# The last token group's products with w_out, taken with tokens on partitions and stored by two queues

## The chip, the cores and the metric

The kernel runs on 1 core of one Trainium2 chip. The metric is device time in microseconds (us) of one execution, lower is better. Before the change the median of 4 runs is 301.98 us (301.85 to 302.33). The profile belongs to one of these runs: it took 302.33 us, of which the profiled span, from the first to the last instruction, is 300.1 us.

## The reference

Two blocks follow each other. The first is a kernelised attention with batch 4, 4 heads, 1088 positions and head size 32: q and k are mapped to 64 features each by an outer product of two small projections, and keys, values and queries are combined through a 64 x 32 matrix per head. Its output, laid out as 4352 tokens of 128 features, is the input x of the second block, a feed-forward layer with 2048 hidden units:

```python
def phi(x):
    a = np.einsum('rd,bhsd->bhsr', S1, x)
    b = np.einsum('rd,bhsd->bhsr', S2, x)
    return np.einsum('bhsi,bhsj->bhsij', a, b).reshape(*x.shape[:-1], r * r)
q_p, k_p = (phi(q), phi(k))
...
h = x @ w_in                                   # 4352 x 128 times 128 x 2048
g = np.where(h > 0.0, h, np.exp(np.minimum(h, 0.0)) - 1.0)
return (g @ w_out).astype(np.float32)          # 2048 x 128
```

## The kernel before

**Tokens and groups.** A sequence of 1088 positions is read as 64 rows y of 17 neighbours t, so position = 17 y + t. A "half tile" is one (batch b, t) with its 64 rows y; there are 4 x 17 = 68 of them. They are taken in 9 groups: groups 0 to 7 have 8 half tiles (512 tokens, as 4 tiles of 128), the last group, g = 8, has 4 half tiles, that is 256 tokens in 2 tiles of 128 (`qn[8] = 2`). In each 128-token tile the upper 64 partitions (u = 0) hold one half tile and the lower 64 (u = 1) another.

**The feed-forward stage.** It takes nearly the whole span. The 2048 hidden units are 16 chunks of 128, worked in 8 pairs (`cp`, `NP = 8`). For each group and pair there is a step:

- `mm1` (L492): two products with w_in give h, hidden units on partitions and tokens on columns, in two PSUM tiles (tag `h`, 4 buffers, line 496). The 128 x 128 piece of w_in is the stationary operand (the one loaded into the array), the group's x (`xg`) the moving one (streamed through).
- `elu` (L514): per chunk, ScalarE makes relu(-h) and exp(-that) (L504, L505), and VectorE combines it with h to `gg` (L511), in SBUF, hidden units on partitions.
- `mm2` (L519): two products with w_out (L525) add into one PSUM tile `o` of the group (tag `o`, one buffer), output features on partitions and tokens on columns. Here too the 128 x 128 piece of `W` is stationary and `gg` (512 columns, 256 in the last group) is moving.

Every float32 product is carried out in two passes, each a weight load and a matmul in the trace; so one `mm2` call has 4 passes.

**The order of the work** is written out by hand: the schedule is manual, and each engine executes its instructions in the order of the emission. The loop over `n` at the end emits `mm1` of step n, then small work of other stages (`extra`), then `elu` of step n, then `mm2` of step n - 2. After the last `mm1` three calls of `mm2` therefore follow each other. Waits between engines go by semaphores that the framework places from the tiles that are read and written, and on TensorE the wait stands ahead of the weight load.

**The end of a group.** `fin1` (L530) takes `o` when its 8 pairs are summed. For groups 0 to 7 VectorE transposes `o` in blocks of 32 x 32 into `ob` (L545) and SyncE's queue stores it in 16 or more small transfers (L551). The last group goes another way: VectorE copies `o` to SBUF as `oT` (L541), and two rounds of the loop later `fin2` (L553) has TensorE transpose its two 128 x 128 tiles (L557) into a PSUM tile of tag `aux`, ScalarE copies that to `osb` (L559), and SyncE's queue issues two transfers, one per half u, of 64 rows of 1 KB (L563): for each y, the 2 neighbouring tokens t, t+1 with 128 features each are contiguous in the output.

Of the kernel before, what the change touches and what calls it, by code (L numbers as in the profile page):

```python
# [12 lines left out]
F32 = mybir.dt.float32  # L13
# [14 lines left out]
def kernel(  # L28
# [18 lines left out]
    nc = tc.nc  # L47
    B, H, S, D = q.shape
    R = S1.shape[0]
    P = 128  # L50
# [3 lines left out]
    NP = NC // 2  # L54
# [7 lines left out]
    work = ctx.enter_context(tc.tile_pool(name="wk", bufs=2))  # L62
    psum = ctx.enter_context(tc.tile_pool(name="psum", bufs=2, space=bass.MemoryType.PSUM))
# [83 lines left out]
    W = const.tile([P, NP, 4 * P], F32, name="W")  # L147
# [49 lines left out]
    ident = const.tile([P, P], F32, name="ident")  # L197
# [138 lines left out]
    NQ = (NH + 7) // 8  # L336
    qn = [min(8, NH - 8 * g) // 2 for g in range(NQ)]
# [5 lines left out]
    def half_tile(g, i, u):  # L343
        return divmod(8 * g + u * qn[g] + i, NT)

    def runs(g, u, i0, i1, step=1):

        i = i0
        while i < i1:
            b, t = half_tile(g, i, u)  # L350
            m = 1
            while i + m * step < i1 and half_tile(g, i + m * step, u)[0] == b:
                m += 1
            yield b, t, i, m
            i += m * step
# [134 lines left out]
    hs, es, gs, ops = {}, {}, {}, {}  # L490

    def mm1(g, cp):  # L492
        n = qn[g] * P
        hs[g, cp] = [psum.tile([P, 512], F32, name="h", tag="h", bufs=4) for c in range(2)]
        for c in range(2):
            nc.tensor.matmul(hs[g, cp][c][:, :n], W[:, cp, c * P:c * P + P], xg[g][:, :n])  # L496
# [17 lines left out]
    def elu(g, cp):  # L514
        for c in range(2):
            elu_a(g, cp, c)
            elu_d(g, cp, c)

    def mm2(g, cp, first, last):  # L519
        n = qn[g] * P  # L520
        if first:
            ops[g] = psum.tile([P, 512], F32, name="o", tag="o", bufs=1)
        gg = gs.pop((g, cp))
        for c in range(2):
            nc.tensor.matmul(ops[g][:, :n], W[:, cp, (2 + c) * P:(3 + c) * P], gg[:, c, :n],  # L525
                             start=(first and c == 0), stop=(last and c == 1))

    oT = {}

    def fin1(g, last):  # L530
        n = qn[g] * P
        o = ops.pop(g)[:, :n]
        if g in oT:
            nc.vector.tensor_add(oT[g][:, :n], oT[g][:, :n], o)
            o = oT[g][:, :n]
        elif not last:
            oT[g] = work.tile([P, 512], F32, name="oT", tag="oT")
            nc.scalar.copy(oT[g][:, :n], o)  # L538
        if last and g == NQ - 1:
            oT[g] = work.tile([P, 512], F32, name="oT", tag="oT")  # L540
            nc.vector.tensor_copy(oT[g][:, :n], o)  # L541
        elif last:

            ob = work.tile([P, 4, 2, 2, D], F32, name="ob", tag="ob", bufs=2)
            nc.vector.transpose(ob[:].rearrange("p i u w d -> p (i u w) d"), o)  # L545
            rows = out.rearrange("(b w y t) (q d) -> b w q y t d", b=B, w=2, t=NT, q=4)
            for u in range(2):
                for b, t, i, m in runs(g, u, 0, qn[g]):
                    for w in range(2):
                        for q_ in range(4):  # L550
                            nc.sync.dma_start(rows[b, w, q_, :, t:t + m, :], ob[32 * q_:32 * q_ + 32, i:i + m, u, w, :])  # L551

    def fin2(g):  # L553
        n = qn[g]
        p = psum.tile([P, 512], F32, name="otp", tag="aux")
        for i in range(n):
            nc.tensor.transpose(p[:, i * P:i * P + P], oT[g][:, i * P:i * P + P], ident[:])  # L557
        o = work.tile([P, 4, P], F32, name="osb", tag="osb", bufs=1)
        nc.scalar.copy(o[:, :n].rearrange("p t f -> p (t f)"), p[:, :n * P])  # L559
        rows = out.rearrange("(b y t) f -> b y t f", b=B, t=NT)  # L560
        for u in range(2):
            for b, t, i, m in runs(g, u, 0, n):
                nc.sync.dma_start(rows[b, :, t:t + m, :], o[64 * u:64 * u + 64, i:i + m, :])  # L563


    keep_warm(2)
# [66 lines left out]
    for b in range(1, B):  # L633

        n = NP - 2 if b == 1 else NP * (b * NT // 8 - 2) + 1
# [10 lines left out]
    for g in range(2, NQ):  # L646
        n = NP * (g - 1) + (g == 2)
# [2 lines left out]
        at(n + 5, q4, g)  # L650
        at(n + 6, q5, g)

    done = {}
    N = len(steps)
    for n in range(N + 4):
        if 2 <= n < N:
            g, cp, first, last = steps[n]
            mm1(g, cp)
        for f, *a in extra.get(n, ()):
            f(*a)  # L660
        if 2 <= n < N:
            elu(g, cp)
        for f, *a in extra.get((n, 1), ()):
            f(*a)
        if 2 <= n < N + 2:
            g, cp, first, last = steps[n - 2]
            mm2(g, cp, first, last)
            if last:
                fin1(g, cp == NP - 1)
                if cp == NP - 1 and g == NQ - 1:  # L670
                    done[n + 2] = g
        if n in done:
            fin2(done[n])


# [27 lines left out]
```

## Time and profile before

| what | value |
|---|---|
| median of 4 runs | 301.98 us (301.85 to 302.33) |
| the profiled execution | 302.33 us, its span 300.1 us |
| TensorE matmul busy | 288.3 us, 96% of the span, 1454 passes |
| VectorE, ScalarE busy | 168.8 us (56%), 188.1 us (63%) |
| products with w_out, L525 | 288 passes, 130.7 us; of these 32 passes of 256 columns in the last group, 8.0 us |
| last pass of L525 ends, VectorE's copy starts | 295.24 us after the start of the span |
| the two last stores are issued | at 296.60 and 297.19 us |

The profile is one execution recorded by the hardware. Times in its views are in us from the start of the span unless they are marked ns. Engines are PE (TensorE's matmuls), PEld (TensorE's weight loads, which overlap PE), DVE (VectorE), ACT (ScalarE), POOL (GpSimd) and SP (SyncE); a q behind a name is its queue of waits and DMA issues. A duration of one matmul in the trace is its latency, from the first column in to the last result out, so neighbours overlap; the distance from start to start is the pace.

### The profile page before, as it was taken

How to read it: one execution, taken by the hardware profiler on the slowest of the kernel's cores; microseconds unless marked ns; L12 is line 12 of the kernel's file. 1: busy time of each engine (PE TensorE's matmuls, PEld its weight loads, DVE VectorE, ACT ScalarE, POOL GpSimd, SP SyncE). 2: the span in 40 equal slices, each digit the busy share in tenths (PEclk: the TensorE clock that was granted, in tenths of full speed). 3: DMA queues.
4: the chain of work that ended last, by engine and by line, in shares of the span. 5: the costliest groups of instructions: out<-in, count | busy, mean ns of one | idle time of the engine just before them, and what ended most of it. 6: DMA issues, size and time to landing. Idle time of an engine off the chain costs nothing.

```text
span 300.1 us, 4046 instructions
## 1 busy us (share of the span) xinstructions
PE 288.3 (96%) x1454; PEld 147.8 (49%) x1454; DVE 168.8 (56%) x297; ACT 188.1 (63%) x354; POOL 18.5 (6%) x45
## 2 busy tenths in 40 slices
PE   8887999999998999999998999999999999999994
PEld 5763335544444654445544654444444534444682
DVE  5788899963765384436356275436443644354441
ACT  1526797566666268746667268656774687568682
POOL 2010024440000010000000010000000000000000
PEclk9999999999999999999999999999999999999998
DMA  6932899620020100001000200001001000110020
GB/s 188 331 127 73 182 209 215 61 74 0 7 31 0 29 9 0 2 9 27 2 1 4 33 0 0 0 15 23 0 0 24 14 0 1 15 22 0 3 33 17
DMA packets 38291, 13.37 MB, mean 45 GB/s; under 512 B 32768, under 2 KB 36480, under 8 KB 38272
## 3 DMA queue, kind: packets, MB, share of 16 engines
q1 hardware_dynamic: 37984, 12.86, 19.7%
q10 hardware_dynamic: 288, 0.26, 0.3%
q8 instruction: 11, 0.18, 0.2%
q14 instruction: 8, 0.07, 0.1%
HBM read 10.88 MB, written 2.23 MB: 44 GB/s over the span
## 4 chain that ended last, share of the span: by engine, by line
PE 92%; ACT 3%; DVE 3%; issue 1%; DVEq 0%
PE o L525 39%; PE h L496 37%; PE kv L296 3%; PE xps L475 2%; PE abp L269 2%; PE idle L216 2%; PE qtp L460 2%; PE abwp L363 2%; ACT e L505 1%; ACT e L504 1%; ACT ab L273 1%; PE x0ps L427 1%; DVE qp L384 0%; PE abqp L394 0%; DVE gg L511 0%
## 5 line engine op out<-in xcount | busy, mean ns | idle before, releaser
L511 DVE SCALAR_TENSOR_TENSOR gg<-e,h 128x512 f32<-128x512 f32 (+1 forms) x144 | 93.0, 656 | 105.8 <-ACT e L505 105.6
L525 PE MATMUL o<-gg,W 128*128 128x512 f32 (+1 forms) x288 | 130.7, 577 | 1.3 <-ACT oT L538 0.7
L496 PE MATMUL h<-xg,W 128*128 128x512 f32 (+1 forms) x288 | 128.8, 569 | 1.8 <-DVE xg L487 0.7
L504 ACT ACTIVATE e<-h 128x512 f32<-128x512 f32 (+1 forms) x144 | 81.5, 566 | 25.4 <-PE h L496 24.9
L505 ACT ACTIVATE e<-e 128x512 f32<-128x512 f32 (+1 forms) x144 | 87.3, 606 | 4.6
L496 PEld LDWEIGHTS h<-xg,W 128*128 128x128 f32 x288 | 54.5, 190 | 65.2 <-issue 55.9
L525 PEld LDWEIGHTS o<-gg,W 128*128 128x128 f32 x288 | 52.2, 190 | 54.8 <-issue 46.4
L368 ACT COPY abw<-abwp 128x384 f32<-128x384 f32 (+1 forms) x8 | 3.7, 459 | 28.4 <-PE abwp L363 28.4
L461 ACT COPY qpT<-qtp 128x512 f32<-128x512 f32 (+1 forms) x16 | 8.2, 562 | 17.1 <-PE qtp L460 17.1
L253 DVE TENSOR_TENSOR kp<-ab 128x1024 f32<-128x1024 f32 (+1 forms) x12 | 11.0, 944 | 5.8 <-ACT ab L273 5.8
L273 ACT COPY ab<-abp 128x256 f32<-128x256 f32 (+1 forms) x12 | 3.8, 317 | 13.3 <-PE abp L269 13.0
L296 PEld LDWEIGHTS kv<-v,kp 128*64 128x64 f32 (+1 forms) x288 | 9.3, 140 | 2.6 <-issue 2.3
L296 PE MATMUL kv<-v,kp 128*64 128x33 f32 (+3 forms) x288 | 10.1, 227 | 0.0
L486 ACT COPY xg<-xps 128x256 f32<-128x256 f32 (+1 forms) x8 | 2.9, 359 | 10.5 <-PE xps L475 10.5
L384 DVE TENSOR_TENSOR qp<-an,abw 128x1024 f32<-128x1024 f32 (+1 forms) x8 | 9.3, 1159 | 0.3
L460 PEld LDWEIGHTS qtp<-ident,qp 128*128 128x128 f32 x60 | 7.0, 143 | 4.0 <-issue 4.0
L269 PE MATMUL abp<-Sab,kT 128*64 128x64 f32 x136 | 7.1, 249 | 1.9 <-ACT ab L273 1.9
L460 PE MATMUL qtp<-ident,qp 128*128 128x128 f32 x60 | 8.0, 274 | 0.6 <-DVE qp L384 0.6
L269 PEld LDWEIGHTS abp<-Sab,kT 128*64 128x64 f32 x136 | 5.8, 159 | 5.4 <-ACT ab L273 2.5
L475 PE MATMUL xps<-qpT,kvS 64*32 64x128 f32 (+2 forms) x200 | 7.6, 298 | 0.3 <-ACT qpT L461 0.3
L316 POOL TENSOR_TENSOR zm<-kvz,zmask 128x32 f32<-128x32 f32 x3 | 1.2, 391 | 108.3 <-issue 65.1
L216 PE MATMUL idle<-some 128*128 128x256 f32 (+1 forms) x16 | 6.6, 558 | 1.2 <-DVE warm L143 1.2
(84 smaller groups left out, 125.9 us busy)
## 6 DMA issues: line engine op xcount, KB each, us to landing
raw<-in_moe_w_in_dram SPq DMA_DIRECT2D x8, 256.0 KB, 5.6
raw<-in_moe_w_out_dram SPq DMA_DIRECT2D x8, 256.0 KB, 6.0
out_dram<-ob SPq DMA_DIRECT2D x104, 16.0 KB, 1.5
hd_k<-in_k_dram SPq DMA_DIRECT2D x3, 544.0 KB, 5.7
hd_q<-in_q_dram SPq DMA_DIRECT2D x3, 544.0 KB, 3.8
v<-in_v_dram SPq DMA_DIRECT2D x12, 72.0 KB, 5.6
v<-in_v_dram SPq DMA_DIRECT2D x12, 64.0 KB, 3.7
hd_k<-in_k_dram SPq DMA_DIRECT2D x1, 288.0 KB, 3.4
```

What stands on the lines that cost most here:

```text
L216: nc.tensor.matmul(idle[:, :cols], some[:, :P], some[:, :cols], skip_group_check=True)
L253: nc.vector.tensor_mul(dst, _ap(a_, list(a_.ap[1:]) + [[0, R]]), _ap(b_, [b_.ap[1], [0, R], b_.ap[2]]))
L269: nc.tensor.matmul(abp[64 * u:64 * u + 64, j * 64:j * 64 + 64], kT[b][:, u * KT + i, :], Sab[:].rearrange("p h y -> p (h y)"), skip_group_ ...
L296: nc.tensor.matmul(kv[64 * hp:64 * hp + 64, g2, :n], kp[:rows, j, h].rearrange("p i j -> p (i j)"), _ap(vt[b][:rows, off:off + D], [[VN - ...
L384: nc.vector.tensor_mul(qp[g][:, :m], _ap(a_, list(a_.ap[1:]) + [[0, R]]), _ap(b_, [b_.ap[1], [0, R], b_.ap[2]]))
L460: nc.tensor.transpose(p[:, o:o + P], qp[g][:, r:r + 2].rearrange("p t i j -> p (t i j)"), ident[:])
L475: nc.tensor.matmul(xp[w][D * h:D * h + D, :nh * P].rearrange("p (m s) -> p m s", s=P)[:, m0:m0 + m, s], kvS[64 * w:64 * w + 64, b, h, :], ...
L496: nc.tensor.matmul(hs[g, cp][c][:, :n], W[:, cp, c * P:c * P + P], xg[g][:, :n])
L504: nc.scalar.activation(e, hs[g, cp][c][:, :n], RELU, scale=-1.0)
L505: nc.scalar.activation(e, e, EXP, scale=-1.0)
L511: nc.vector.scalar_tensor_tensor(gs[g, cp][:, c, :n], es[g, cp][:, c, :n], -1.0, hs[g, cp][c][:, :n], op0=ADD, op1=MAX)
L525: nc.tensor.matmul(ops[g][:, :n], W[:, cp, (2 + c) * P:(3 + c) * P], gg[:, c, :n], start=(first and c == 0), stop=(last and c == 1))
```

## The change

The last group alone is changed. Its `mm2` is replaced by `mm2_last`: `gg` is now the stationary operand, 128 tokens at a time, and the 128 x 128 piece of w_out the moving one. The result comes out with tokens on partitions and features on columns, in two PSUM tiles `ol` of 128 x 128, one in the buffer of tag `o` and one in a buffer of tag `aux`. In the last of the 8 pairs the order of the four products is changed, so that the first token tile is finished ahead of the second. The copy to `oT`, the two transposes and the copy to `osb` are gone. `fin_last`, after the loop, copies the first token tile by ScalarE and the second by VectorE into one SBUF tile, and issues the two transfers, of the same shape as before, one on SyncE's queue and one on ScalarE's. The loop has two rounds fewer at its end; those held only `fin2`.

```diff
@@ fin1
-        if last and g == NQ - 1:
-            oT[g] = work.tile([P, 512], F32, name="oT", tag="oT")
-            nc.vector.tensor_copy(oT[g][:, :n], o)
-        elif last:
+        if last:
...
-    def fin2(g):
-        n = qn[g]
-        p = psum.tile([P, 512], F32, name="otp", tag="aux")
-        for i in range(n):
-            nc.tensor.transpose(p[:, i * P:i * P + P], oT[g][:, i * P:i * P + P], ident[:])
-        o = work.tile([P, 4, P], F32, name="osb", tag="osb", bufs=1)
-        nc.scalar.copy(o[:, :n].rearrange("p t f -> p (t f)"), p[:, :n * P])
+    def mm2_last(cp, first, last):
+        g = NQ - 1
+        if first:
+            ops[g] = [psum.tile([P, P], F32, name="ol", tag=t, bufs=k) for t, k in (("o", 1), ("aux", 2))]
+        gg = gs.pop((g, cp))
+        for a in range(4):
+            c, i = (a % 2, a // 2) if last else divmod(a, 2)
+            nc.tensor.matmul(ops[g][i][:], gg[:, c, i * P:i * P + P], W[:, cp, (2 + c) * P:(3 + c) * P],
+                             start=(first and c == 0), stop=(last and c == 1))
+
+    def fin_last():
+        g, n = NQ - 1, qn[NQ - 1]
+        o = work.tile([P, 2, P], F32, name="ol", tag="ol", bufs=1)
         rows = out.rearrange("(b y t) f -> b y t f", b=B, t=NT)
-        for u in range(2):
-            for b, t, i, m in runs(g, u, 0, n):
-                nc.sync.dma_start(rows[b, :, t:t + m, :], o[64 * u:64 * u + 64, i:i + m, :])
+        for i, copy in enumerate((nc.scalar.copy, nc.vector.tensor_copy)):
+            copy(o[:, i, :], ops[g][i][:])
+        for u, eng in enumerate((nc.sync, nc.scalar)):
+            b, t = half_tile(g, 0, u)
+            eng.dma_start(rows[b, :, t:t + n, :], o[64 * u:64 * u + 64])
...
-    for n in range(N + 4):
+    for n in range(N + 2):
...
             g, cp, first, last = steps[n - 2]
-            mm2(g, cp, first, last)
-            if last:
-                fin1(g, cp == NP - 1)
-                if cp == NP - 1 and g == NQ - 1:
-                    done[n + 2] = g
-        if n in done:
-            fin2(done[n])
+            if g == NQ - 1:
+                mm2_last(cp, first, last)
+            else:
+                mm2(g, cp, first, last)
+                if last:
+                    fin1(g, cp == NP - 1)
+    fin_last()
```

More of the change, by code (lines that the diff above doesn't have):

```diff
@@ L651 @@
         at(n + 6, q5, g)
-    done = {}
     N = len(steps)
-    for n in range(N + 4):
+    for n in range(N + 2):
         if 2 <= n < N:
```

## The prediction

> **What bounds the kernel now.** I read the page's chain of waits first. TensorE carries it nearly alone, so a cost counts if it lies on TensorE or behind TensorE's last product.
>
> ```profile
> PE 92%; ACT 3%; DVE 3%; issue 1%; DVEq 0%
> ```
>
> Next I asked for the same chain in order of time, for the last 17 us (start, us, what). It shows the last three calls of `mm2` as 12 passes in a row, and behind them a relay through three engines that nothing overlaps.
>
> ```profile
> 291.75 0.86 PE h L496 x4
> 292.62 2.60 PE o L525 x12
> 295.22 0.02 issue
> 295.24 0.44 DVE oT L541
> 295.68 0.04 issue
> 295.72 0.46 PE otp L557 x2
> 296.18 0.02 issue
> 296.20 0.37 ACT osb L559
> ```
>
> What follows is in the timeline of SyncE's queue and in the table of waits of that queue. The two stores are issued one behind the other, 0.55 and 0.60 us each (the durations of the two in the tile's own view, 549 and 596 ns), so the second starts at 297.19. Each lands 2.0 us after its issue, about 298.6 and 299.2, and at the end SyncE waits for both of them: 1.2 us in two waits.
>
> ```profile
> 296.60 1.19 SPq L563 DMA_DIRECT2D out_dram<-osb  x2
> DMA to landing us min/median/max: 2.0/2.0/2.0
> SPq L699 <- DMA out_dram<-osb: 1.2, 2, 0.6
> ```
>
> The time from the last landing to the end of the span, 300.1 - 299.2 = 0.9 us, and the 302.33 - 300.1 = 2.2 us around the span stay as they are. Up to the first `mm2` of the last group, at 283.71, the list of each engine's instructions is the same before and after; I cost all of that at nothing.
>
> **Part 1, the passes on TensorE.** Before, the last group has 8 calls x 2 products x 2 passes = 32 passes of 256 columns. From start to start they take (2.75 - 0.379) / 11 = 0.2155 us, from the row below of the 12 last passes and the 379 ns of one. After, there are 8 x 4 x 2 = 64 passes of 128 columns, each with its own load of 128 x 128 weights. The columns streamed are the same; the weight loads are twice as many. All of it lies on the path. The question is the pace of a 128-column pass with a new float32 weight each time, and three places of the trace bound it (start, us, engine, line, operation, tiles, count):
>
> ```profile
> 292.45 2.75 PE L525 MATMUL o<-gg,W 128*128 128x256 f32 x12
> 16.82 0.97 PEld L427 LDWEIGHTS x0ps<-kvz,qpT 128*128 128x128 f32 x8
> 18.68 0.30 PEld L216 LDWEIGHTS idle<-some 128*128 128x128 f32 x2
> 267.98 0.60 PE L460 MATMUL qtp<-ident,qp 128*128 128x128 f32 x4
> ```
>
> L427 loads the same 128 x 128 float32 weights for only 66 columns, so there the loads set the pace: (0.97 - 0.192) / 7 = 0.111 us. L216 in its 128-column form has our shape: its second load starts 0.30 - 0.19 = 0.11 us behind the first, and one matmul streams meanwhile. L460, transposes of 128 columns, has (0.60 - 0.273) / 3 = 0.109 us. So loads and streams of 128 are about equal, and they overlap. Half of the old pass, 0.108, is the lower end (no cost). The upper end is the duration of one such load, 0.190 us, as if loads did not overlap each other. I take 0.111, of the row that is bound by loads of this kind: 64 x 0.111 - 32 x 0.2155 = 7.10 - 6.90 = **+0.2 us** (ends: 0 and 64 x 0.190 - 6.90 = +5.3).
>
> The Trainium skill has a rule against this: "TensorE: Matmul & The Clock Gate", Part 3, The mechanism, says that a weight load overlaps a running matmul only when it targets another row group; ours use all rows. By it a pass would be load plus stream, 0.111 + 0.108 = 0.22 us, and the part 64 x 0.22 - 6.90 = +7.2 us; the 0.2155 us of the 256-column passes, each with a load of 128 x 128, leaves no room for such an addition.
>
> Two waits move. `gg` is now loaded, not streamed, so it is wanted one pass earlier. In the steady state it is ready more than 1 us ahead; at the end it is close. VectorE's last `gg` ends at 293.81 + 0.42 = 294.23, plus 0.15 for the slower passes of the five calls before. The load that wants it is that of the third of the last eight passes. It comes 17 paces after the run's start at 292.45 + 0.15, at 294.49. The cover is about 0.1 us; if it is gone the delay is that overrun and one exposed load, 0.1 us. I take nothing. The wait of the first call for the buffer of tag `o` (VectorE's transpose of group 7) is there before and after; the `aux` buffer was last read by the copies at 272.5 and is free.
>
> **Part 2, the relay.** Gone are VectorE's copy of 256 columns, the transposes and ScalarE's copy: from VectorE's start at 295.24 to the issue at 296.60 it is 1.36 us. In their place one copy of 128 x 128 stands behind the last pass. ScalarE's copy of the first token tile starts four passes earlier (0.44 us) and takes 0.27, so it is hidden; without that cover it would cost 0.1 at most, since it runs beside VectorE's. Prices are those of two copies of this shape:
>
> ```profile
> 272.49 0.27 ACT L486 COPY xg<-xps 128x128 f32<-128x128 f32 x1 [1.13 <-PE xps L475]
> 272.53 0.29 DVE L487 COPY xg<-xps 128x128 f32<-128x128 f32 x1 [0.46 <-PE xps L475]
> ```
>
> The last pass itself: with 23 paces of 0.111 the last one starts 2.55 us into the run, and a 128-column pass is read by the next engine about 0.31 us after its start (the second transpose: from 295.72 + 0.44 - 0.27 = 295.89 to ScalarE's start at 296.20). That gives 2.86, against 295.24 - 292.45 = 2.79 before; 0.05 of it is in part 1 already, so I count 0.02 here. Then 0.29 us for the copy and 0.05 for the two queues to see it, since both issues now wait for VectorE and ScalarE. The relay shrinks from 1.36 to 0.36: **-1.0 us**. Both stores are issued near 295.8 (295.24 + 0.2 + 0.36).
>
> **Part 3, the stores.** Nothing is queued behind them: SyncE's earlier stores are issued by 291.5, and ScalarE has no other work left. Before, the second store is issued 0.59 us after the first. After, both start together, and -0.59 us is the most that can be won. Against it, two sets of data arrive at the same 16 DMA engines. From both sides: nothing (they interleave), or all 0.59, if issue and data follow each other. The start of the kernel has the nearest row, where SyncE and ScalarE each issue one transfer 0.16 us apart (288 and 256 KB). In the DMA view of the 1.0 us that follow the first packet only SyncE's queue (q1) moves data; ScalarE's (q10) begins when q1 has moved most of its own:
>
> ```profile
> q1 hardware_dynamic: 157, 0.18, 83.2%
> ...
> q1 hardware_dynamic: 115, 0.11, 55.2%
> q10 hardware_dynamic: 110, 0.11, 52.7%
> ```
>
> The first line is the window 2.6 to 3.6, the others 3.6 to 4.2. So I let the data follow each other: 80 packets of about 59 ns over 16 engines are 0.3 us (42.1% of 16 engines over 1.4 us for both stores is 9.4 us of packets, 0.29 us per store and engine). I take **-0.29 us** (ends -0.59 and 0). ScalarE may also be slower to issue: its first issue of the kernel took 590 ns where SyncE's, of the same size, took 406; that adds at most 0.18.
>
> The skill's page "DMA: Bandwidth & Descriptors", Rules for kernel authors, advises against splitting a transfer by partition halves or spreading it over queues, since they share the same 16 engines and only issue time is saved. Here the split exists already, and issue time, 0.59 us, is what stands to be won; no row before the change shows two stores at once.
>
> **The sum:** +0.2 - 1.0 - 0.29 = -1.1 us. Of the profiled execution's 302.33 us that leaves 301.25. The median of the runs shown is 0.35 lower than that execution, so I forecast **300.9 us**, 0.36% faster. Best ends: passes at 0.108 (-0.2) and no contention (-0.3) give 300.4. Worst ends within the forecast: stores one after the other (+0.29), the slow issue (+0.18) and the late `gg` (+0.1) give 301.5.
>
> **The rivals.**
>
> 1. *The stores do not run side by side.* For: the start-up rows above, and 16 engines that both share. Against: those were transfers four times as large. The gain is then the relay alone, +0.2 - 1.0, with the slow issue -0.6 to -0.8: 301.2 to 301.4.
> 2. *The weight loads set the pace, slower than the nearest rows say* (TensorE, the 64 passes). For: one load lasts 190 ns in the trace, more than the 108 ns of its stream, and `gg` has never been the loaded operand here. Against: L427's eight loads in a row, each 0.19 us long and 0.111 apart. At 0.190 the time is 300.9 + 64 x (0.190 - 0.111) = 306.0. The gain behind the passes is 1.3 us, so it decides from a pace of 0.108 + 1.3 / 64 = 0.128 us; at 0.138 the kernel is slower by 0.2%. At 0.12 to 0.138 there would be no clear difference.
> 3. *It doesn't do what it says.* The list of the built program's instructions has the 32 products of 128 x 128, no transpose and no `oT`, one last store on SyncE and one on ScalarE. I give this nothing.
>
> **How the numbers follow.** 0.2% of 301.98, 0.6 us, is about what a measurement of this kernel can tell from no change. The forecast with its ends has 0.78, all of it faster. Rival 1 has 0.10, 0.08 of it faster, 0.02 the same. Rival 2 has 0.06 slower, and a pace in between, the same, 0.06. Faster 0.86, same 0.08, slower 0.06. The range 300.4 to 301.5 holds the forecast and rival 1, and leaves out rival 2.
>
> **What will show it.** Right: 64 passes of the new line, eight in about 0.89 us, with no idle time ahead of their loads; the last pass ends about 295.5; one copy of 0.29 us on VectorE; two issues within 0.1 us near 295.8, on two queues; the last landing near 298.1, the span near 299.0. Wrong: passes 0.13 us apart or more; loads that wait for `gg`; a q10 that begins only when q1 is done and lands past 298.5; or an issue on ScalarE well behind SyncE's.

## The result, and the profile after

The changed kernel takes 301.34 us (median of 46 runs, 300.44 to 304.59) against 302.06 us before (67 runs, 301.44 to 304.87). The ratio is 0.9977, with a 95% interval of 0.9966 to 0.9988: faster, by 0.7 us (0.36 to 1.03 us). The forecast was 300.9 us and 1.1 us less than before.

Its profiled execution took 301.65 us, with a span of 299.4 us. The page's chain of waits is still TensorE's:

```profile
PE 90%; DVE 3%; ACT 3%; DMA 2%; issue 1%; SPq 0%; DVEq 0%
```

Here is the end of its chain of waits in order of time (start, us, what):

```profile
292.26 0.87 PE h L496 x4
293.12 2.69 PE ol L558 x24
295.81 0.02 issue
295.84 0.29 DVE ol L566
```

Of the relay through VectorE, TensorE and ScalarE one copy of 0.29 us is left. The 24 passes of the last three calls take 2.69 us, 0.112 each, where the 12 before took 2.60. The group of the new products, by form, in the last 15 us (matmuls, then their weight loads: busy us, mean ns of one, and the idle time before them):

```profile
L558 PE MATMUL ol<-W,gg 128*128 128x128 f32 x64 | 8.2, 276 | 0.0
L558 PEld LDWEIGHTS ol<-W,gg 128*128 128x128 f32 x64 | 8.0, 192 | 0.6 <-DVE ob L542 0.3
```

The 64 passes have no idle time ahead of them, and the one wait ahead of a load is that for VectorE's transpose of group 7, which was there before too. No load waits for `gg`. The timeline and the DMA view of the last microseconds show the two stores (issue; then KB each and us from issue to landing):

```profile
296.19 0.55 SPq L569 DMA_DIRECT2D out_dram<-ol  x1
296.20 0.56 ACTq L569 DMA_DIRECT2D out_dram<-ol  x1
```

```profile
out_dram<-ol SPq DMA_DIRECT2D x1, 64.0 KB, 2.0
out_dram<-ol ACTq DMA_DIRECT2D x1, 64.0 KB, 2.3
```

Both are issued together, ScalarE's no slower than SyncE's. In the DMA view SyncE's queue (q1) is alone at first, from 297.38 to 297.7, and ScalarE's (q10) alone at last, from 297.9 to 298.2 (packets, MB, share of 16 engines); ScalarE's first packet starts at 297.70, 0.15 us ahead of the end of SyncE's last.

```profile
q1 hardware_dynamic: 59, 0.06, 83.7%
...
q10 hardware_dynamic: 36, 0.02, 31.5%
```

So the data follow each other for the most part, as forecast.

In the table of waits of SyncE's queue the two waits for landings, 1.2 us together before, are one:

```profile
SPq L704 <- DMA out_dram<-ol: 1.5, 1, 1.5
```

SyncE's store lands in 2.0 us as before, ScalarE's 0.27 us later, at 298.48. The issues, the last landing and the end of the span are each about 0.4 us later than the prediction's "What will show it" names them. Of that, 0.36 comes from ahead of the last group, as the next paragraph shows.

**The tail as a measure.** The time up to the last group varies from execution to execution, so I compare profiles by their tails: from the start of the `mm1` right ahead of the last group's first product with w_out to the end of the span. In the timelines of before and after that start is the row

```profile
282.74 1.03 PE L496 MATMUL h<-xg,W 128*128 128x256 f32 x4
```

```profile
283.10 1.03 PE L496 MATMUL h<-xg,W 128*128 128x256 f32 x4
```

The tail was 300.06 - 282.74 = 17.32 us and is 299.38 - 283.10 = 16.28 us: 1.04 us less, where the forecast's sum was about 1.1 (0.2 - 1.0 - 0.29 = -1.09). But the changed kernel's tail starts 0.36 us later, although TensorE, VectorE and ScalarE execute the same instructions in the same order up to there. Whether that lateness belongs to the change was the first question.

| run | tail starts | tail | against before | median, us | ratio (95%) |
|---|---|---|---|---|---|
| before | 282.74 | 17.32 | | 302.06 | |
| after | 283.10 | 16.28 | -1.04 | 301.34 | 0.9977 (0.9966 to 0.9988) |
| e1, changed kernel again | 282.36 | 16.28 | -1.04 | 301.16 | 0.9964 (0.9946 to 0.9982) |
| e2, new products, one queue | 285.32 | 16.57 | -0.75 | 301.36 | 0.9987 (0.9959 to 1.0014) |
| e3, old products, two queues | 282.81 | 16.91 | -0.41 | 301.62 | 0.9990 (0.9966 to 1.0015) |
| e4, before again | 282.27 | 17.34 | +0.02 | 302.25 | 0.9999 (0.9976 to 1.0022) |
| e5, four stores | 282.71 | 16.30 | -1.02 | 301.40 | 0.9987 (0.9961 to 1.0012) |
| e6, order not swapped | 282.80 | 16.28 | -1.04 | one run | |
| e7, one bank, one copy | 282.75 | 16.25 | -1.07 | one run | |
| e8, products of 64 columns | 282.68 | 23.38 | +6.06 | one run | |
| e9, both copies on VectorE | 282.98 | 16.21 | -1.11 | 301.26 | 0.9971 (0.9951 to 0.9990) |

The "before" medians beside e1 to e4, e5 to e8 and e9 were 302.05, 302.08 and 302.12 us. A tail repeats within 0.02 us (before and e4, after and e1); the median of a kernel moves by 0.2.

### The profile page after: what moved, and what is told of

It reads as the page before. It is cut to its first block, busy times and chain, and to the rows that moved or that the text cites. A ratio compares the mean times of both kernels' runs of the same rounds, so it can differ in the third digit from the quotient of the medians.

```text
span 299.4 us, 4107 instructions
## 1 busy us (share of the span) xinstructions
PE 288.1 (96%) x1484; PEld 148.7 (50%) x1484; DVE 169.0 (56%) x297; ACT 188.0 (63%) x354; POOL 18.5 (6%) x45
## 4 chain that ended last, share of the span: by engine, by line
PE 90%; DVE 3%; ACT 3%; DMA 2%; issue 1%; SPq 0%; DVEq 0%
PE o L525 37%; PE h L496 37%; PE kv L296 3%; PE ol L558 2%; PE xps L475 2%; PE qtp L460 2%; PE abwp L363 2%; DMA hd_q<-in_q_dram 2%; PE abp L269 2%; ACT e L505 1%; ACT e L504 1%; ACT ab L273 1%; PE x0ps L427 1%; PE idle L216 0%; DVE qp L384 0%
## 5 line engine op out<-in xcount | busy, mean ns | idle before, releaser
L525 PE MATMUL o<-gg,W 128*128 128x512 f32 x256 | 122.7, 602 | 1.3 <-ACT oT L538 0.7
L525 PEld LDWEIGHTS o<-gg,W 128*128 128x128 f32 x256 | 46.2, 190 | 53.7 <-issue 46.4
L558 PEld LDWEIGHTS ol<-W,gg 128*128 128x128 f32 x64 | 8.0, 192 | 0.6 <-DVE ob L542 0.3
L558 PE MATMUL ol<-W,gg 128*128 128x128 f32 x64 | 8.2, 276 | 0.0
```

Of the source, the lines that this page charges most:

```text
L558: nc.tensor.matmul(ops[g][i][:], gg[:, c, i * P:i * P + P], W[:, cp, (2 + c) * P:(3 + c) * P], start=(first and c == 0), stop=(last and c ...
```

## The experiments

**e1, the changed kernel again.** No edit. "First pass" in this expectation lies 0.97 us behind the start of the tail in the table, so its 15.3 us is a tail of 16.27. The tails that e2 and e3 expect are counted from that pass too: 15.65 us is 16.62 in the table, 16.0 is 16.97.

> The changed kernel once more. Theory A (the change acts only behind the first product of the last group; the 0.36 us by which the changed kernel's profile is late ahead of that point is the spread of the first loads from run to run): from the last group's first pass with w_out to the end of the span 15.3 us against 16.35 us before, so a ratio near 0.9965 (-1.06 us); the start of that pass can be anywhere from 283.5 to 284.1 us. Theory B (something in the changed program makes the start-up itself later, always by about 0.3 us): that pass starts again near 284.07 us, in every kernel with the new tail, and the ratio is near 0.9977 (-0.7 us).

Measured: the first pass starts at 283.33 us, not at 284.07; the tail is 16.28 us, the same as in the first profile to 0.01; the ratio is 0.9964. Theory B falls: this execution is 0.74 us earlier at the same point of the same program.

**e4, the kernel before again.** No edit.

> The kernel before once more, for the spread. Ratio 1.000 within its interval. Theory A: the start of the last group's first pass with w_out differs from 283.71 us by up to 0.3 us; theory B: it is within 0.1 us of 283.71.

Measured: tail 17.34 us, start 282.27, which is 0.47 us earlier than in the first profile of the same kernel, more than I had allowed. The old tail's profiles start at 282.74, 282.81 and 282.27, the new tail's, without e2's, at 282.36 to 283.10: the two overlap. Theory A stands.

Most of the spread arises in the first 12 us. Against the first profile of the kernel before, TensorE is by then 0.47 us early in e1, 0.53 early in e4 and 0.22 late in the changed kernel's first profile, whose other 0.14 us arise between there and 80 us. In that profile the chain leads back to the load of q, which lands at 7.23 us (5.98 to 6.24 in the ten other profiles), in e2's to the load of v (start, us, what):

```profile
1.90 5.33 DMA hd_q<-in_q_dram
```

```profile
3.90 6.38 DMA v<-in_v_dram
```

**e2, the new products with one queue.**

```diff
-        for u, eng in enumerate((nc.sync, nc.scalar)):
+        for u, eng in enumerate((nc.sync, nc.sync)):
```

> The changed kernel with both last stores on SyncE's queue. Both theories: the second store is issued 0.59 us after the first and lands 2.05 us later, 0.34 us behind the changed kernel's last landing. Tail 15.65 us. Theory A: ratio near 0.9976 (-0.7 us), start of the last group's first pass with w_out anywhere from 283.5 to 284.1. Theory B: that start near 284.07 and a ratio near 0.999 (-0.35 us). If instead two queues give the whole issue time back (rival: stores interleave), the loss is 0.6 us.

Measured: tail 16.57 us, 0.05 less than expected. The second queue is worth 0.28 us on top of the new products, where I expected 0.34, and the new products alone give 0.75. The timeline of SyncE's queue has both issues in a row again:

```profile
298.42 1.19 SPq L569 DMA_DIRECT2D out_dram<-ol  x2
```

The ratio, 0.9987, can't tell this kernel from no change. Its profiled execution is one of those that are 3 us longer, 304.16 us; what happened there is told at the end.

**e3, the old products with two queues.**

```diff
-                nc.sync.dma_start(rows[b, :, t:t + m, :], o[64 * u:64 * u + 64, i:i + m, :])
+                (nc.sync, nc.scalar)[u].dma_start(rows[b, :, t:t + m, :], o[64 * u:64 * u + 64, i:i + m, :])
```

> The kernel before with its second last store on ScalarE's queue instead of SyncE's; products, transposes and copies as before. Both theories: the last landing 0.34 us earlier, tail 16.0 us against 16.35, ratio near 0.9989. The start of the last group's first pass with w_out: anywhere in 283.5 to 284.1 by theory A; near 283.7 by theory B, since the tail's new tiles are not there.

Measured: tail 16.91 us, 0.41 to 0.43 us less than with one queue, where I expected 0.34. In the old kernel the second queue is worth more than the 0.28 us it adds to the new products. The DMA view shows that here the other store came first:

```profile
out_dram<-osb SPq DMA_DIRECT2D x1, 64.0 KB, 2.2
out_dram<-osb ACTq DMA_DIRECT2D x1, 64.0 KB, 2.0
```

The last landing is 2.2 us after the issue instead of 2.3. And SyncE's last two waits stand in a fixed order, the semaphore of ScalarE's store first. In the trace's semaphore events of the changed kernel the first of them ends at 298.50 and the second follows 0.06 us later, on the path to the end; here the second ends with its own landing, and no other wait for a landing follows. Together that is 0.13 us, the difference between 0.41 and 0.28.

**e5, four stores by token tile.**

```diff
-        o = work.tile([P, 2, P], F32, name="ol", tag="ol", bufs=1)
+        os = [work.tile([P, P], F32, name=f"ol{i}", tag=f"ol{i}", bufs=1) for i in range(2)]
...
-            copy(o[:, i, :], ops[g][i][:])
-        for u, eng in enumerate((nc.sync, nc.scalar)):
-            b, t = half_tile(g, 0, u)
-            eng.dma_start(rows[b, :, t:t + n, :], o[64 * u:64 * u + 64])
+            copy(os[i][:], ops[g][i][:])
+            for u, eng in enumerate((nc.sync, nc.scalar)):
+                b, t = half_tile(g, i, u)
+                eng.dma_start(rows[b, :, t, :], os[i][64 * u:64 * u + 64])
```

> The changed kernel, but each token tile has an SBUF tile and two stores of its own (64 rows of 512 B, one on each queue), so the first tile's stores are issued while the second tile's products and copy are still running. In the changed kernel the last landing comes 2.30 us after the issue instead of 2.0 to 2.07, because the data of the second store follow those of the first. Theory A1 (the extra 0.25 to 0.3 us are bytes): only half the data are left behind the last copy, which costs 0.15 us instead of 0.3; each queue is busy with its first issue until 0.05 to 0.1 us after the last copy; net -0.1 us, tail from the last group's mid step 16.2 us against 16.28. Theory A2 (packets, not bytes: each packet costs the same 50 ns): as many packets stand behind the last copy as before, nothing is won and the late second issue costs 0.05 to 0.1 us: 16.35 us. Time about the changed kernel's, ratio 0.996 to 0.998.

Measured: tail 16.30 us, 0.02 more than the changed kernel's; its median is 301.40. The first tile's stores go out early, at 295.29, and the issues of the second tile's follow at once (the two rows cover two issues each):

```profile
295.29 1.20 SPq L569 DMA_DIRECT2D out_dram<-ol  x2
295.30 1.47 ACTq L569 DMA_DIRECT2D out_dram<-ol  x2
```

The packets doubled from the changed kernel's 160, as the DMA view of the end counts them:

```profile
DMA packets 320, 0.13 MB, mean 44 GB/s; under 512 B 64, under 2 KB 320, under 8 KB 320
```

So nothing was won, but not for A2's reason. In the trace's semaphore events the last landing comes 2.12 us after the second issues, against 2.29 in the changed kernel: fewer bytes behind the last copy do land 0.17 us sooner, as A1 has it, although there are as many packets. The second issues come late, at 295.95, 0.21 us behind the end of the last copy (295.45 + 0.29 = 295.74 in the timeline) instead of 0.06, since each queue is still busy with its first. I had allowed 0.05 to 0.1 for that. SyncE also has two more waits behind the one that ends last, where the changed kernel has one, which adds 0.04 us. What the data give, the later issue and the waits take.

**e6, the order of the last pair not swapped.**

```diff
-            c, i = (a % 2, a // 2) if last else divmod(a, 2)
+            c, i = divmod(a, 2)
```

> The changed kernel with the last pair's four products in the order of the other pairs. The first token tile is then finished two passes (0.22 us) instead of four (0.45 us) before the second; ScalarE's copy of 0.27 us ends 0.05 us after the last pass, ahead of VectorE's, which ends 0.29 us behind it. Expected: no change of the tail (16.28 us, within 0.03) - the swap was not needed for this cover. Rival: the copy's end sets the stores' issue, then +0.05 us or more.

Measured: tail 16.28 us. The timeline shows the first tile's copy inside the cover, 0.25 us ahead of the other's end:

```profile
295.31 0.27 ACT L566 COPY ol<-ol 128x128 f32<-128x128 f32 x1 [1.33 <-PE ol L558]
295.54 0.29 DVE L566 COPY ol<-ol 128x128 f32<-128x128 f32 x1 [1.10 <-PE ol L558]
```

**e7, one PSUM tile and one copy.**

```diff
-            ops[g] = [psum.tile([P, P], F32, name="ol", tag=t, bufs=k) for t, k in (("o", 1), ("aux", 2))]
+            ops[g] = psum.tile([P, 2, P], F32, name="ol", tag="o", bufs=1)
...
-            nc.tensor.matmul(ops[g][i][:], gg[:, c, i * P:i * P + P], W[:, cp, (2 + c) * P:(3 + c) * P],
-                             start=(first and c == 0), stop=(last and c == 1))
+            nc.tensor.matmul(ops[g][:, i, :], gg[:, c, i * P:i * P + P], W[:, cp, (2 + c) * P:(3 + c) * P],
+                             start=(first and a == 0), stop=(last and c == 1), skip_group_check=True)
...
-        for i, copy in enumerate((nc.scalar.copy, nc.vector.tensor_copy)):
-            copy(o[:, i, :], ops[g][i][:])
+        nc.vector.tensor_copy(o[:], ops[g][:])
```

> The changed kernel with both token tiles in one PSUM tile and one VectorE copy of 256 columns at the end, ScalarE copies nothing. It measures what the split of the copy is worth: 0.425 us (the copy of 256 columns) instead of 0.292, so +0.13 us, tail 16.41 us. Passes stay 0.1116 us apart. Rival: two copies into one SBUF tile cost the wait for both semaphores (0.04 us), then only +0.09 us.

A miss: the tail is 16.25 us, 0.04 less, not 0.13 more. The copy is longer as expected, but the stores are issued sooner behind it (295.49 + 0.43 = 295.92, issue at 295.94):

```profile
295.49 0.43 DVE L565 COPY ol<-ol 128x256 f32<-128x256 f32 x1 [1.10 <-PE ol L558]
295.94 0.56 SPq L568 DMA_DIRECT2D out_dram<-ol  x1
```

From the copy's end to the issue it is 0.03 us with one engine to wait for and 0.06 with two. The rest is the same effect as in e3: ScalarE's store landed first (2.0 against 2.2 us), and no other wait follows the last landing.

**e8, products of 64 columns.** Each product of the last group is cut in two; all of the work is done.

```diff
-            nc.tensor.matmul(ops[g][i][:], gg[:, c, i * P:i * P + P], W[:, cp, (2 + c) * P:(3 + c) * P],
-                             start=(first and c == 0), stop=(last and c == 1))
+            for f in (0, 64):
+                nc.tensor.matmul(ops[g][i][:, f:f + 64], gg[:, c, i * P:i * P + P],
+                                 W[:, cp, (2 + c) * P + f:(2 + c) * P + f + 64],
+                                 start=(first and c == 0 and f == 0), stop=(last and c == 1), skip_group_check=True)
```

> The changed kernel with every product of the last group cut in two of 64 columns of w_out: 128 passes instead of 64, the same columns streamed, twice the loads of gg. If the load of 128 x 128 float32 weights sets the pace (0.1116 us whatever is streamed beside it): 128 x 0.1116 = 14.3 us instead of 7.1, +7.1 us. If the stream sets it and loads are hidden: 128 x 0.055 = 7.0, no change. If load and stream follow each other: 128 x (0.111 + 0.054) = 21 us, +14 us.

Measured: tail 23.38 us, 7.10 more than the changed kernel's. The end of its chain:

```profile
297.17 5.32 PE ol L559 x48
302.49 0.02 issue
302.51 0.29 DVE ol L568
```

Twice the loads with the same columns streamed take twice the time, 5.32 us for 48 passes, 0.111 each. The load of 128 x 128 float32 weights sets the pace, and the stream beside it is hidden. A fixed time for each pass, whatever it loads, would look the same in e8. The profile before rules it out: 16 passes of L363, which load weights of 64 columns and stream 96, take 0.81 us, 0.05 each.

```profile
17.93 0.81 PE abwp L363 x16
```

**e9, both copies on VectorE.**

```diff
-        for i, copy in enumerate((nc.scalar.copy, nc.vector.tensor_copy)):
+        for i, copy in enumerate((nc.vector.tensor_copy, nc.vector.tensor_copy)):
```

> The changed kernel with both final copies on VectorE (the first token tile's copy 0.45 us earlier, hidden as ScalarE's was). The two stores then wait for one engine less: in the run with one copy the issue came 0.027 us behind the copy's end, with two engines 0.063 us. Expected by the theory that the wait for a second engine costs issue time and brings the two issues 13 instead of 4 ns apart: issue 0.04 us earlier and the last landing up to 0.06 us sooner, tail 16.15 to 16.25 us against 16.28, ratio 0.996. Rival: the first copy delays the second on VectorE or the landing is set by the data of the two queues alone, then 16.24 or more.

Measured: tail 16.21 us, 0.07 less than the changed kernel's. The issue comes 0.04 us earlier, and the last landing is sooner by the rest:

```profile
295.27 0.29 DVE L566 COPY ol<-ol 128x128 f32<-128x128 f32 x1 [0.66 <-PE ol L558]
295.71 0.29 DVE L566 COPY ol<-ol 128x128 f32<-128x128 f32 x1 [0.15 <-PE ol L558]
296.03 0.56 SPq L569 DMA_DIRECT2D out_dram<-ol  x1
```

It has the shortest tail of all. In whole times, 301.26 us against 301.16 and 301.34, it can't be told from the changed kernel.

## Why the prediction was right, point by point

- **Part 1, the passes: +0.2 us.** Right in pace and size. In the trace the passes start 0.1116 us apart, by 64 it is 7.14 us, and VectorE's last copy starts 12.74 us into the tail against 12.50 before, +0.24. The row that decided was L427's eight loads, and e8 shows that the reading, loads set the pace, is the right one.
- **The rule against it.** A load that could not overlap a running matmul of the same rows, as the Trainium skill's "TensorE: Matmul & The Clock Gate", Part 3, The mechanism, has it, would have made e8's passes load plus stream, over 0.16 us. They were 0.111. For these loads the rule does not hold. The same section also lets a load into a background weight buffer be pulled ahead of running matmuls; whether that is what happens here no run shows.
- **The moved waits: nothing.** Right: no pass of the last group waits for `gg`, and e6, which wants it two passes later, ends at the same time. The cover, forecast as 0.1 us, was 0.12: the last `gg` ends at 294.73, the load that wants it starts at 294.86.
- **Part 2, the relay: -1.0 us.** Right. From VectorE's start to the first issue it was 1.36 us and is 296.19 - 295.84 = 0.35. (The 0.02 us that the forecast added for the last pass were in part 1 already: 24 of the 64 passes carry 0.08 of its 0.21 us.) The cover of ScalarE's copy is larger than needed (e6). The split over two engines makes the copy 0.13 us shorter, but adds 0.03 us of waiting and came with the less favourable order of the two stores, so that against one copy (e7) it gains nothing; the split by tile on one engine (e9) is 0.03 us shorter than one copy, from one profile each.
- **Part 3, the stores: -0.29 us.** The size is right, 0.28 by e2, partly by luck. The last landing comes 2.64 us after the first issue with one queue (e2) and 2.29 with two, 0.36 sooner: of the issue time of 0.59 us, 0.24 comes back because the second store's data land after the first's, where the forecast had 0.3. The other 0.07 lies behind the last landing, which the forecast left at 0.9 us: it was 0.83 and is 0.90, since SyncE's wait for the last landing now has another wait behind it. The slower issue on ScalarE did not come (0.56 us). The Trainium skill's "DMA: Bandwidth & Descriptors", Rules for kernel authors, says that only the sequencer's issue time is saved by a second queue; the runs agree, and add that 0.31 of the 0.59 us came back at the landing and the waits behind it.
- **The sum.** The parts make -1.09 us and the tails show -1.04. The measured medians differ by 0.72, the ratio by 0.36 to 1.03 us, and in e1's runs by 0.89 and 0.54 to 1.63 us. So the mechanism was right, and 301.34 us lies in the range, but the whole time shows some 0.3 us less gain than the tail in the first comparison. The start-up does not explain it. It varies by 0.8 us between executions and made the changed kernel's first profile 0.36 us late, but the starts of seven profiles with the new tail (e2's left out) average 282.77, those of three with the old 282.61, within their spread. And the medians of the spans are 298.8 us for the changed kernel (the first comparison's executions, and e1's) and 299.8 for the kernel before (81 executions, those run beside the experiments and e4's): 1.0 us less, as the tails have it. Nearly half of what is missing lies outside the span, which the forecast had as 2.2 us and unchanged: its median is 2.4 us in the first comparison's executions of the changed kernel, and 2.3 in e1's and in those of the kernel before. The kernel is the same in both, so the change does not make it; what does is not shown. The rest is no more than the 0.2 us by which medians move.
- **The rivals.** Rival 1 (nothing from the second queue) had 301.2 to 301.4 us, so the measured 301.34 alone would fit it better than the forecast of 300.9; it fell by e2 and e3. Rival 2 (slow loads) fell by the pace.

## What to carry to other kernels

When the last tile of a matrix product leaves through a transpose, making it with the operands exchanged gives the wanted layout at once. The price is the number of weight loads: at 128 columns the load of float32 weights and the stream are equally long, so the exchange costs nearly nothing there, and twice the time at 64 columns. A second queue for the last store gives back the issue time less the time by which the data follow each other, here 0.28 to 0.43 of 0.59 us. For a change worth less than the spread of the start-up, compare the profile from the point where the programs part: here that repeated within 0.02 us, where whole medians needed dozens of runs to see 0.7.

## What the runs showed that I had not expected

Some executions take some 3 us more, and it has nothing to do with the change: the kernel before has them too, up to 304.99 us. One of them left a profile, e2's (304.16 us). There the last load of v lands at 10.27 us, no later than in others (10.17 before, 10.58 in the changed kernel's first profile). But TensorE had done its earlier work by 8.9 and waited 1.5 us for v, so that it was busy for only 0.42 of the 2 us from 8 to 10. At 11.0 us the granted clock went down to half; it is 0.50 and 0.53 in the two stretches of 2 us after those shown, and full again after 17.9 us. The table of stretches of e2 (stretch, its length, busy us of PE, PEld, DVE, ACT, POOL, granted clock, DMA share, GB/s):

```profile
8.00:10.00 2.00, 0.42 (x6) 0.19 (x2) 2.00 (x4) 0.64 (x4) 0.00 (x0) 1.00 1.05 246
10.00:12.00 2.00, 1.59 (x33) 1.51 (x34) 1.82 (x3) 0.49 (x1) 0.00 (x0) 0.76 1.10 357
12.00:14.00 2.00, 2.00 (x9) 1.67 (x10) 1.09 (x3) 0.76 (x2) 0.00 (x0) 0.50 1.06 365
```

In e4's profile the wait at this place is shorter, 0.87 us, TensorE is busy for 0.67 us of the same stretch, and the clock stays at 1.00 in this one and in all that follow it up to 24 us:

```profile
8.00:10.00 2.00, 0.67 (x16) 0.42 (x11) 2.00 (x3) 0.84 (x3) 0.00 (x0) 1.00 1.07 272
```

When the products with v start, e2's execution is 0.1 us behind the first profile of the kernel before (10.41 against 10.30), at 20 us 2.55: nearly all of the loss falls into the 7 us of halved clock. That the wait brought the clock down is an inference from these two profiles. It is not the only cause of long executions: seven others on record have a mean clock of 0.986 to 0.989, where e2's has 0.987, but two are as long at 0.998 and 1.000 (304.23 and 304.59 us), and they left no profile.

The other surprise is that of two stores issued 4 to 13 ns apart either can land first. Where SyncE's issue is 12 or 13 ns ahead (the changed kernel, e1, e6, e8) SyncE's store did; where it is 4 or 5 ns ahead, ScalarE's did in e3 and e7 and SyncE's in e9. It moves the end by about 0.1 us.
